# A second group of filler matmuls, and a new set of ranks, in a hand-scheduled attention and feed-forward kernel

## The chip, the core and the metric

The kernel runs on one core of one Trainium2 chip. The metric is the device time of one execution in microseconds; the median of several runs counts. A profile comes from one further execution, taken by the hardware profiler, with its own time.

The engines are named as in the profile: PE is TensorE (matmuls; PEld its weight loads), DVE is VectorE, ACT is ScalarE, POOL is GpSimd, SP is SyncE, which issues loads and stores. Each takes its instructions strictly in the order in which the program was built, and waits where an instruction's inputs or buffers aren't ready.

## What is computed

Attention over selected chunks of keys, and a gated feed-forward network (FFN) on its output, in float32 from and to memory:

```python
# q, k, v: (4, 8, 768, 64); chunks of 32 keys, 24 of them; the best 6 per query
ub = sum_d max(q * k_min[chunk], q * k_max[chunk])     # bound of a chunk, causal chunks only
top = argsort(ub)[..., -6:]
scores = q @ k.T / 8, masked to the keys of `top` and to earlier positions
attn = softmax(scores);  x = (attn @ v) as (3072, 512)
xn = x / rms(x) * rms_g
out = (silu(xn @ w_gate) * (xn @ w_val)) @ w_out       # 512 -> 1536 -> 512
```

## The kernel before

**Pairs.** The 32 heads (4 batches of 8) are taken as 16 pairs of heads, p = 0 to 15; a batch is four pairs. For each pair `prep` loads k and q (`knat`, `qnat`, issued on SP), transposes them on PE (`kT` and `qT`: tiles `pk`, `pq`, L498), copies them out (`kt`, `qt`, on ACT or DVE), reduces the chunks' maxima and minima on DVE (L524, L526, and `ku` on POOL or DVE), multiplies them for the bounds (`ub`, L586), transposes back (`up`, L610), finds the sixth largest bound on DVE (`ubm`, `max`, `selq`, to L644), transposes the selection (`st`, L655) and copies it into the lower rows of the query operand (`qs`). With these rows, and a pattern beside the keys, the score matmul itself adds a large negative number for keys that aren't selected.

**Scores.** `scores` goes through a pair's two heads in groups of at most four 128x128 blocks: score matmuls into PSUM (`sc`, L718, for the first batch with a matmul on a triangular mask, L724), exp on ACT (`pt`, L735), product with v (`av`, L754), and normalisation on DVE into `xb` (L769, L770). The fourth pair (p = 3) is done in two halves of the sequence, so that the first half of the first batch can go on early.

**FFN.** For each half of a batch `norm` takes sums of squares (`sq`, on ACT or DVE), adds epsilon (`ms`, DVE, L810), takes the root on POOL (L818), scales three tiles of 128 rows on DVE (`xs`, L826), and transposes them; in the first batch on PE (`tp`, L848) with a copy by ACT or DVE (`xT`), in the others by DMA. `ffn` then does 12 times a gate matmul (`gp`, four instructions, L882), tanh on ACT (`sg`), a product on DVE (`tg`), a val matmul (`vp`, four instructions, L903) and a product on DVE (`hh`); then nine parts of the output matmul (`po`, four instructions each, L923), evictions and stores. The weights `wg`, `wv` and `wo` are loaded in two halves each, issued on POOL.

**Fillers.** At the start PE has little to do. 48 matmuls of 512 columns on a tile of zeros (`busy`, L341) can be placed there; nobody reads what they write.

**Order.** No scheduler runs on the chip. Before the program is emitted, `Order.run` plays all steps through with estimated durations: at each moment an idle engine takes, among the steps whose inputs and buffers are ready, the one with the lowest rank. The sequence in which the steps were taken is the order of every engine's instructions. A step's rank is a sum: of its kind (the table `RANK`, for the first batch and for the others), of its place (the table `TIMES`: `s3.0` for the scores of the fourth pair's first half, `f0.0` for the first FFN half, and so on) and of a pace times its number within the place. The tables were found by a search. The fillers have rank 1000 and more, behind nearly everything: the planner places one only where PE would have nothing else.

```python
    for i in range(BUSY):
        bank = Buf("ps")
        add("busy", "PE", pe(4 * P), 1000.0 + i, busy(bank), [c_zero], opens=[bank])
```

Of the kernel before, what the change touches and what calls it, by code (L numbers as in the profile page):

```python
# [24 lines left out]

RANK = (
    dict(
        av=156.13, dif=-333.01, eps=-30.9, exp=-297.75, kC=249.04, kE=-171.16, kT=-97.43,
        kload=1.5, kmn=-85.09, kmx=75.56, max=-238.74, qC=324.63, qE=-109.16, qT=-140.07,
        qload=45.82, relu=246.29, root=261.37, sc=129.21, sel=17.88, selC=51.2, selT=55.02,  # L30
        sq=-363.37, tp=-68.78, tpE=108.05, ub=-155.85, ubE=-484.91, ubm=-159.09, up=-350.79,
        vload=-102.18, xb=-100.78, xs=-3.48,
    ),
    dict(
        av=8.1, dif=164.62, eps=-549.11, exp=227.88, gate=-37.01, hh=-145.73, kC=-36.47,
        kE=243.85, kT=-61.3, kload=39.2, kmn=324.05, kmx=284.92, mask=143.91, max=194.96,
        out=-122.32, po=137.5, poE=216.04, qC=234.68, qE=-450.99, qT=88.22, qload=32.32,
        relu=163.99, root=-883.1, sc=-22.64, sel=-113.94, selC=20.01, selT=-328.58, sq=384.43,
        tanh=51.44, tg=-50.58, ub=10.99, ubE=298.61, ubm=-119.37, up=-28.2, val=-0.94,
        vload=151.14, xT=-62.62, xb=39.12, xs=-64.22,  # L40
    ),
)

TIMES = {
# [15 lines left out]
}  # L60


# [139 lines left out]
def kernel(  # L202
# [11 lines left out]
    nc = tc.nc  # L214
    P = nc.NUM_PARTITIONS
# [25 lines left out]
    WHOLE, HALVES = [(0, NT)], [(0, HB), (HB, HB)]  # L241
    PARTS = [WHOLE] * 3 + [HALVES] + [WHOLE] * (NPAIRS - NP)
    FIRST = 42.0
    BUSY = 48
    LIMITS = dict(score=(5, 3), av=(2, 2), prep=(4, 3), ffn=(3, 4), norm=(3, 2), po=(2, 2))
    order = Order(SLOTS, limits)
    order.LIM = LIMITS
# [3 lines left out]
    def add(name, engs, occ, rank, *a, **kw):  # L251
        return order.add(name, engs, occ, rank if isinstance(rank, dict) else {"": rank}, *a, **kw)
# [14 lines left out]
    ps = ctx.enter_context(tc.tile_pool(name="ps", bufs=1, space=PSUM))  # L267
# [11 lines left out]
    def act(n):  # L279
        return 0.065 + n * 0.00083  # L280
# [4 lines left out]
    def pool(n):  # L285
        return 0.22 + n * 0.00085

    def pe(n):
        return 0.003 + n / 2400.0
# [36 lines left out]
    def make_ident(e):  # L326
# [7 lines left out]
        out=first[:], in_=ident_f[:, 0:1], func=ACT.Exp), [c_id])  # L334
    zeros = const.tile([P, 4 * P], BF16, name="zeros")
    c_zero = add("zeros", "DVE", 0.2, -101, lambda e: nc.vector.memset(zeros[:], 0.0))

    def busy(bank):
        def go(e):
            t = tile_of(bank, [P, 4 * P], FP32, "busy")  # L340
            nc.tensor.matmul(t[:], zeros[:, 0:P], zeros[:], start=True, stop=True)  # L341
        return go

    for i in range(BUSY):
        bank = Buf("ps")
        add("busy", "PE", pe(4 * P), 1000.0 + i, busy(bank), [c_zero], opens=[bank])
    c_ku = [add("ku0", "DVE", 0.1, -95 + i, lambda e, i=i: nc.vector.memset(KU[i][:], 0.0))
            for i in range(SLOTS["ku"])]
    c_sel = [add("selq0", "DVE", 0.38, -90 + i, lambda e, i=i: nc.vector.memset(SELQ[i][:], 0.0))
# [52 lines left out]
    def make_tri(e):  # L402
# [10 lines left out]
        out=gains[:], in_=moe_rms_g.rearrange("(o n) -> o n", o=1).to_broadcast([P, DM])),  # L413
# [279 lines left out]
    def scores(c, i0, nb, at, pace, adds):  # L693
        p, b = c.p, c.b
        if b not in XB:
            XB[b], XBS[b] = Buf("xb"), {}
        for hl in range(2):
            kk = slice(0, KM) if hl == 0 else slice(0, P)
            av = Buf("ps", "av")
# [3 lines left out]
            for g, (nd, regions) in enumerate(groups):  # L703
                sc, pt = Buf("ps", "score"), Buf("pt")
                nn = sum(x[2] for x in regions)
                todo, x = [], 0
                for kb, q0, y in regions:
                    todo += [(x + j, kb, q0 + j) for j in range(y)]
                    x += y
                m = g + hl * len(groups)  # L710
                tri = nd if adds else 0

                def score(e, regions=regions, sc=sc, hl=hl, kk=kk, tri=tri):
                    t = tile_of(sc, [P, 4, P], FP32, "sc")
                    ke, qs = KE[c.set.slot][hl], QS[c.set.slot][hl]
                    x = 0
                    for kb, q0, m in regions:
                        nc.tensor.matmul(  # L718
                            t[:, x:x + m, :].rearrange("p a b -> p (a b)"),
                            ke[kk, kb * P:(kb + 1) * P], qs[kk, q0 * P:(q0 + m) * P],  # L720
                            start=not tri or x == 0, stop=not tri)
                        x += m
                    if tri:
                        nc.tensor.matmul(  # L724
                            t[:, 0:tri, :], ident_b[:],
                            trimask[:].rearrange("p (o q) -> p o q", o=1).to_broadcast([P, tri, P]),
                            start=False, stop=True)

                need = list(c.sel) + [y for z in c.ke.values() for y in z] + [c_tri] + c_ke
                s = add("sc", "PE", sum(pe(x[2] * P) for x in regions) + (pe(tri * P) if tri else 0),  # L730
                        rank(at, b, "sc", m, pace), score, need, opens=[sc], uses=[c.set])

                def soft(e, sc=sc, pt=pt, nn=nn):
                    t = tile_of(pt, [P, 4, P], BF16, "pt")
                    nc.scalar.activation(out=t[:, 0:nn, :], in_=sc.tile[:, 0:nn, :], func=ACT.Exp,  # L735
                                         scale=SCALE)

                x = add("exp", "ACT", act(nn * P), rank(at, b, "exp", m, pace), soft, [s], opens=[pt], uses=[sc])
                if nd and not adds:
                    def mask(e, pt=pt, nd=nd):  # L740
                        nc.gpsimd.affine_select(  # L741
                            out=pt.tile[:, 0:nd, :], in_=pt.tile[:, 0:nd, :],
                            compare_op=ALU.is_ge, fill=0.0, base=0,
                            pattern=[[0, nd], [1, P]], channel_multiplier=-1)

                    x = add("mask", "POOL", pool(nd * P), rank(at, b, "mask", m, pace), mask, [x], uses=[pt])

                def prod(e, pt=pt, todo=todo, av=av, left=left, hl=hl):
                    begin = av.tile is None
                    if begin:  # L750
                        tile_of(av, [P, nb, D + 1], FP32, "av")
                    left[0] -= 1
                    for m, (x, kb, qi) in enumerate(todo):
                        nc.tensor.matmul(  # L754
                            av.tile[:, qi - i0, :], pt.tile[:, x, :],
                            VX[c.v.slot][:, hl * NT + kb, :],
                            start=(begin and m == 0), stop=(left[0] == 0 and m == len(todo) - 1))

                avs.append(add("av", "PE", 0.029 * nn, rank(at, b, "av", m, pace), prod, [x, c.vload], opens=[av],
                               uses=[pt, c.v]))  # L760

            def norm_out(e, hl=hl, av=av):
                if XB[b].tile is None:
# [10 lines left out]
            s = add("xb", "DVE", 0.30 + nb * 64 * 0.00104, rank(at, b, "xb", (hl + 1) * len(groups), pace),  # L774
                    norm_out, avs, opens=[XB[b]], uses=[av])
# [210 lines left out]
```

## Time and profile before

| | us |
|---|---|
| median of 3 runs | 325.68 (325.23 to 325.82) |
| the profiled execution | 326.77 |
| its span, first to last instruction | 325.1 |
| mean granted TensorE clock over the span | 0.989 of full |
| first FFN matmul starts | 56.06 |
| last matmul ends | 321.1 |

The page of the profile gives the busy time of each engine, and the span in 40 equal slices of 8.13 us, each digit a tenth; in its row PEclk a 9 is the full granted clock. Busy time of PE includes the latency of each matmul, so two matmuls that follow each other overlap in the records, and a lone one looks longer than what it takes from the array. A view by stretches gives busy time, clock and DMA for chosen windows; the chain of waits follows the work that ended last back from the end, and there a run of matmuls stands with the time that it added; a timeline lists instructions in order, with the idle time before them and its cause in brackets.

### The profile page before, as it was taken

How to read it: one execution, taken by the hardware profiler on the slowest of the kernel's cores; microseconds unless marked ns; L12 is line 12 of the kernel's file. 1: busy time of each engine (PE TensorE's matmuls, PEld its weight loads, DVE VectorE, ACT ScalarE, POOL GpSimd, SP SyncE). 2: the span in 40 equal slices, each digit the busy share in tenths (PEclk: the TensorE clock that was granted, in tenths of full speed). 3: DMA queues.
4: the chain of work that ended last, by engine and by line, in shares of the span. 5: the costliest groups of instructions: out<-in, count | busy, mean ns of one | idle time of the engine just before them, and what ended most of it. 6: DMA issues, size and time to landing. Idle time of an engine off the chain costs nothing.

```text
span 325.1 us, 7875 instructions
## 1 busy us (share of the span) xinstructions
PE 316.8 (97%) x2972; PEld 200.5 (62%) x2972; DVE 245.1 (75%) x664; ACT 201.5 (62%) x434; POOL 118.8 (37%) x170
## 2 busy tenths in 40 slices
PE   8999998999999999999999999999999999999995
PEld 3567865667667767765667667556665466555542
DVE  6789988799789889879998767969767778444500
ACT  5578988575777498993469779755465252333121
POOL 8649426364425764583213556520012000000000
PEclk9999997899999999999999999999999999999999
DMA  9999999798908669857010330150000720011023
GB/s 172 213 216 198 180 198 219 118 191 143 92 0 184 87 106 169 149 140 50 1 50 2 24 28 2 40 123 35 0 2 33 131 65 1 34 65 66 1 79 114
DMA packets 92501, 30.25 MB, mean 93 GB/s; under 512 B 85424, under 2 KB 89264, under 8 KB 92464
## 3 DMA queue, kind: packets, MB, share of 16 engines
q1 hardware_dynamic: 62352, 21.50, 29.8%
q0 software_dynamic: 28512, 7.87, 24.0%
q10 hardware_dynamic: 1600, 0.39, 0.6%
q8 instruction: 23, 0.38, 0.5%
q14 instruction: 14, 0.11, 0.1%
HBM read 28.57 MB, written 6.29 MB: 107 GB/s over the span
## 4 chain that ended last, share of the span: by engine, by line
PE 92%; DVE 4%; DMA 1%; ACT 1%; issue 0%; ACTq 0%
PE gp L882 20%; PE vp L903 19%; PE po L923 19%; PE sc L718 11%; PE av L754 6%; PE ub L586 5%; PE pq L498 3%; PE pk L498 3%; PE busy L341 3%; PE up L610 2%; PE st L655 2%; DMA qnat<-in_q_dram 1%; DVE selq L644 1%; PE tp L848 0%; DVE selq L639 0%
## 5 line engine op out<-in xcount | busy, mean ns | idle before, releaser
L735 ACT ACTIVATE pt<-sc 128x512 bf16<-128x512 f32 (+3 forms) x192 | 90.9, 570 | 7.4 <-PE sc L718 5.2
L889 ACT ACTIVATE sg<-gp 128x384 bf16<-128x384 f32 x96 | 46.9, 493 | 53.1 <-PE gp L882 52.3
L882 PE MATMUL gp<-xT,wg 128*128 128x384 bf16 x384 | 76.1, 331 | 0.0
L903 PE MATMUL vp<-xT,wv 128*128 128x384 bf16 x384 | 75.7, 326 | 0.0
L895 DVE SCALAR_TENSOR_TENSOR tg<-sg,gp 128x384 bf16<-128x384 bf16 x96 | 51.7, 550 | 25.7 <-ACT sg L889 24.8
L923 PE MATMUL po<-wo,hh 128*128 128x512 bf16 x288 | 69.2, 379 | 0.0
L911 DVE TENSOR_TENSOR hh<-vp,tg 128x384 bf16<-128x384 f32 x96 | 52.3, 553 | 9.7 <-PE vp L903 8.6
L718 PE MATMUL sc<-qs,ke 89*128 89x128 bf16 (+5 forms) x420 | 56.7, 256 | 0.5 <-ACT qs L294 0.4
L882 PEld LDWEIGHTS <-wg 128*128 128x128 bf16 x384 | 36.9, 99 | 25.2 <-issue 2.4
L903 PEld LDWEIGHTS <-wv 128*128 128x128 bf16 x384 | 36.0, 98 | 23.1 <-issue 0.8
L741 POOL TENSOR_SCALAR_AFFINE_SELECT pt<-pt 128x512 bf16<-128x512 bf16 (+1 forms) x48 | 26.1, 556 | 63.3 <-ACT pt L735 62.8
L923 PEld LDWEIGHTS <-hh 128*128 128x128 bf16 x288 | 27.3, 98 | 26.7
L754 PE MATMUL av<-vx,pt 128*128 128x65 bf16 x672 | 38.9, 193 | 1.3 <-ACT pt L735 1.3
L754 PEld LDWEIGHTS <-pt 128*128 128x128 bf16 x672 | 32.4, 98 | 10.6 <-ACT pt L735 2.2
L718 PEld LDWEIGHTS <-ke 89*128 89x128 bf16 (+1 forms) x420 | 30.9, 99 | 10.2 <-issue 2.1
L298 POOL CAST qs<-qt 64x768 bf16<-64x768 f32 x30 | 28.3, 944 | 24.3 <-DVE qt L298 13.3
L298 POOL CAST ke<-kt 64x768 bf16<-64x768 f32 x31 | 26.5, 855 | 8.3 <-ACT kt L294 5.9
L296 ACT ACTIVATE osb<-po 128x512 f32<-128x512 f32 x19 | 11.3, 597 | 29.2 <-PE po L923 29.2
L294 ACT ACTIVATE qs<-st 64x768 bf16<-64x768 bf16 x20 | 16.1, 804 | 7.5 <-PE st L655 7.2
L826 DVE SCALAR_TENSOR_TENSOR xs<-xb,ri,gains 128x512 bf16<-128x512 bf16 x24 | 18.3, 797 | 1.5 <-DMA xT<-xs 1.0
L770 DVE TENSOR_TENSOR xb<-av,rden 128x384 bf16<-128x384 f32 (+1 forms) x34 | 18.2, 534 | 1.2
L631 DVE MAX8 m<-ubm 128x8 f32<-128x24 f32 x192 | 18.9, 169 | 0.1
(72 smaller groups left out, 335.8 us busy)
## 6 DMA issues: line engine op xcount, KB each, us to landing
out_dram<-osb SPq DMA_DIRECT2D x24, 256.0 KB, 2.2
knat<-in_k_dram SPq DMA_DIRECT2D x30, 192.0 KB, 4.8
qnat<-in_q_dram SPq DMA_DIRECT2D x30, 192.0 KB, 4.9
vx<-in_v_dram POOLq DMA_DIRECT2D x16, 192.0 KB, 5.2
wo<-in_moe_w_out_dram POOLq DMA_DIRECT2D x2, 768.0 KB, 9.3
wg<-in_moe_w_gate_dram POOLq DMA_DIRECT2D x2, 768.0 KB, 8.8
wv<-in_moe_w_val_dram POOLq DMA_DIRECT2D x2, 768.0 KB, 9.3
ke<-e_all SPq DMA_DIRECT2D x4, 96.0 KB, 3.4
```

Source lines behind the costliest of these rows:

```text
L298: engine[e].tensor_copy(out_, in_)
L498: nc.tensor.transpose(t[:, j * P:(j + 1) * P], nat[w].tile[:, j0 + j].rearrange("p h d -> p (h d)"), ident_f[:])
L718: nc.tensor.matmul(t[:, x:x + m, :].rearrange("p a b -> p (a b)"), ke[kk, kb * P:(kb + 1) * P], qs[kk, q0 * P:(q0 + m) * P], start=not tri ...
L735: nc.scalar.activation(out=t[:, 0:nn, :], in_=sc.tile[:, 0:nn, :], func=ACT.Exp, scale=SCALE)
L741: nc.gpsimd.affine_select(out=pt.tile[:, 0:nd, :], in_=pt.tile[:, 0:nd, :], compare_op=ALU.is_ge, fill=0.0, base=0, pattern=[[0, nd], [1, ...
L754: nc.tensor.matmul(av.tile[:, qi - i0, :], pt.tile[:, x, :], VX[c.v.slot][:, hl * NT + kb, :], start=(begin and m == 0), stop=(left[0] == ...
L882: nc.tensor.matmul(t[:], wg[:, g, hs], XT[b].tile[:, g, cols], start=(g == 0), stop=(g == NP - 1))
L889: nc.scalar.activation(out=t[:], in_=gp.tile[:], func=ACT.Tanh, scale=0.5)
L895: nc.vector.scalar_tensor_tensor(out=t[:], in0=sg.tile[:], scalar=1.0, in1=gp.tile[:], op0=ALU.add, op1=ALU.mult)
L903: nc.tensor.matmul(t[:], wv[:, g, hs], XT[b].tile[:, g, cols], start=(g == 0), stop=(g == NP - 1))
L911: nc.vector.tensor_tensor(out=t[:], in0=vp.tile[:], in1=tg.tile[:], op=ALU.mult)
L923: nc.tensor.matmul(po.tile[:], hhs[ht].tile[:, th * P:(th + 1) * P], wo[:, ht, :], start=(ht == 0), stop=(ht == NHT - 1))
```

## The change

There are two parts. After the scores of the third pair (p = 2) forty more matmuls on zeros are offered to the planner, of 256 columns each. They depend on the pair's last score step and on nothing else, have the same ranks of 1000 and more as the first group, and each takes a PSUM bank for the time that it runs. And both rank tables hold new numbers, from a new search with these forty in place; by them every engine's order changes from the second pair on. All steps are the same; the eviction copies that either ACT or DVE may do are shared out differently.

```diff
 RANK = (
     dict(
-        av=156.13, dif=-333.01, eps=-30.9, exp=-297.75, kC=249.04, kE=-171.16, kT=-97.43,
+        av=144.2, dif=-491.58, eps=80.61, exp=-371.37, kC=299.85, kE=4.76, kT=-114.77,
...
 TIMES = {
-    "a0": -160.49, "a1": -10.55, "a10": 206.64, "a11": 125.99, "a12": 264.8, "a13": 190.02,
+    "a0": -265.54, "a1": 7.97, "a10": 278.72, "a11": 147.3, "a12": 324.93, "a13": 250.5, "a14":
...
-    BUSY = 48
+    BUSY, LATER = 48, 40
...
-    def busy(bank):
+    def busy(bank, n):
         def go(e):
             t = tile_of(bank, [P, 4 * P], FP32, "busy")
-            nc.tensor.matmul(t[:], zeros[:, 0:P], zeros[:], start=True, stop=True)
+            nc.tensor.matmul(t[:, 0:n], zeros[:, 0:P], zeros[:, 0:n], start=True, stop=True)
         return go
...
-        add("busy", "PE", pe(4 * P), 1000.0 + i, busy(bank), [c_zero], opens=[bank])
+        add("busy", "PE", pe(4 * P), 1000.0 + i, busy(bank, 4 * P), [c_zero], opens=[bank])
...
-                s = add("sc", "PE", sum(pe(x[2] * P) for x in regions) + (pe(tri * P) if tri else 0),
+                s = last_sc = add("sc", "PE", sum(pe(x[2] * P) for x in regions) + (pe(tri * P) if tri else 0),
                         rank(at, b, "sc", m, pace), score, need, opens=[sc], uses=[c.set])
...
+            if p == 2 and hl:
+                for i in range(LATER):
+                    bank = Buf("ps")
+                    add("busy", "PE", pe(2 * P), 1000.0 + i, busy(bank, 2 * P), [last_sc], opens=[bank])
```

More of the change, by code (lines that the diff above doesn't have):

```diff
@@ L27 @@
     dict(
-        av=156.13, dif=-333.01, eps=-30.9, exp=-297.75, kC=249.04, kE=-171.16, kT=-97.43,
[L29 to L32, printed above, removed]
+        av=144.2, dif=-491.58, eps=80.61, exp=-371.37, kC=299.85, kE=4.76, kT=-114.77,
+        kload=9.63, kmn=30.2, kmx=-28.41, max=-225.53, qC=341.63, qE=-85.17, qT=-65.07,
+        qload=37.04, relu=227.01, root=185.03, sc=127.33, sel=95.16, selC=107.08, selT=-124.54,
+        sq=-359.31, tp=-102.27, tpE=5.42, ub=-213.91, ubE=-563.24, ubm=167.25, up=-358.34,
+        vload=-60.34, xb=-160.93, xs=-122.34,
     ),
     dict(
[L35 to L40, printed above, removed]
+        av=-11.76, dif=-2.19, eps=-312.61, exp=84.27, gate=-33.95, hh=-312.21, kC=-56.83,
+        kE=197.29, kT=-62.54, kload=46.97, kmn=412.42, kmx=172.58, mask=54.76, max=242.91,
+        out=-348.43, po=91.59, poE=382.1, qC=107.93, qE=-401.84, qT=31.34, qload=43.39,
+        relu=98.28, root=-755.08, sc=-47.74, sel=57.49, selC=-254.04, selT=-245.0, sq=236.73,
+        tanh=185.25, tg=-53.7, ub=-43.58, ubE=291.78, ubm=15.41, up=-21.92, val=-11.75,
+        vload=304.71, xT=30.46, xb=28.85, xs=-150.44,
     ),
```

28 rows, old and new, of the table TIMES are left out of this document.

## The prediction

> **What bounds the kernel now.** I read the page first: which engine is full, and where its clock was not.
>
> ```profile
> span 325.1 us, 7875 instructions
> PE 316.8 (97%) x2972; PEld 200.5 (62%) x2972; DVE 245.1 (75%) x664; ACT 201.5 (62%) x434; POOL 118.8 (37%) x170
> PEclk9999997899999999999999999999999999999999
> ```
>
> TensorE (PE) is busy 97% of the span, and the granted clock falls in one place only, the seventh and eighth of the 40 slices (48.8 to 65.0 us). The busy time by stretches narrows that down; after the stretch's length come the busy time of PE, PEld, DVE, ACT and POOL, each with its count, then the clock, the DMA share and GB/s.
>
> ```profile
> 48.00:49.00 1.00, 0.44 (x7) 0.15 (x3) 0.77 (x5) 1.00 (x6) 0.00 (x1) 1.00 1.14 199
> 49.00:50.00 1.00, 0.56 (x7) 0.32 (x7) 0.97 (x4) 1.00 (x4) 1.00 (x2) 1.00 1.16 202
> 50.00:51.00 1.00, 0.60 (x8) 0.36 (x9) 1.00 (x3) 0.54 (x2) 0.94 (x2) 1.00 1.16 202
> 51.00:52.00 1.00, 0.87 (x10) 0.62 (x11) 1.00 (x2) 0.45 (x1) 1.00 (x1) 1.00 1.16 202
> 52.00:53.00 1.00, 0.63 (x8) 0.59 (x7) 1.00 (x2) 0.98 (x2) 1.00 (x2) 0.62 1.16 201
> 53.00:54.00 1.00, 1.00 (x6) 0.51 (x5) 0.47 (x1) 1.00 (x3) 0.01 (x1) 0.50 1.15 211
> 54.00:58.00 4.00, 4.00 (x23) 2.58 (x22) 2.49 (x8) 3.85 (x10) 1.64 (x3) 0.50 1.25 239
> 58.00:59.00 1.00, 1.00 (x5) 0.48 (x4) 0.55 (x1) 0.21 (x2) 0.24 (x1) 0.50 1.15 200
> 59.00:60.00 1.00, 1.00 (x8) 0.57 (x7) 0.55 (x1) 0.80 (x3) 0.00 (x0) 0.97 1.15 201
> 56.06:60.00 3.94, 3.94 (x17) 1.96 (x16) 2.31 (x6) 2.95 (x9) 0.87 (x1) 0.62 1.17 208
> 60.00:305.56 245.56, 245.56 (x2282) 156.50 (x2281) 196.11 (x508) 152.45 (x333) 83.21 (x114) 1.00 0.41 68
> ```
>
> From 48 to 53 us PE idles 0.56 + 0.44 + 0.40 + 0.13 + 0.37 = 1.90 us. The clock then goes to half and stays there until 59: lost time 0.38 + 0.50 + 2.00 + 0.50 + 0.03 = 3.41 us, 3.94 x 0.38 = 1.50 us of it after 56.06. From 60 us to the final stretch PE never idles. So after the feed-forward part (FFN) starts, at 56.06, the end is a matter of PE work alone; before it, of the chain that feeds the first gate. The chain that ended last and the engines' timelines (start, length) show that chain:
>
> ```profile
> 49.14 0.27 PE L754 MATMUL av<-vx,pt 128*128 128x65 bf16 x3 [0.70 <-ACT pt L735]
> 51.64 0.40 PE L848 MATMUL tp<-ident_b,xs 128*128 128x128 bf16 x4
> 52.41 1.86 PE L718 MATMUL sc<-qs,ke 89*128 89x128 bf16 x10 [0.37 <-ACT qs L294]
> 54.92 0.63 PE L848 MATMUL tp<-ident_b,xs 128*128 128x128 bf16 x4
> 56.06 4.22 PE L882 MATMUL gp<-xT,wg 128*128 128x384 bf16 x16
> 305.56 15.55 PE po L923 x72
> 48.74 0.17 DVE L810 TENSOR_SCALAR ms<-ss 128x3 f32<-128x3 f32 x1 [0.23 <-ACT junk L797]
> 50.84 2.63 DVE L826 SCALAR_TENSOR_TENSOR xs<-xb,ri,gains 128x512 bf16<-128x512 bf16 x3
> 55.59 0.42 DVE L298 COPY xT<-tp 128x512 bf16<-128x512 bf16 x1
> 53.08 0.58 ACT L294 ACTIVATE xT<-tp 128x512 bf16<-128x512 bf16 x1
> ```
>
> The three scaled rows (xs) are done at 53.47, yet the third transpose (tp) starts only at 54.92, behind scores at half clock, its copy ends at 56.01, and the gate starts at 56.06. PE ends at 321.1; evicting and storing the last tile takes the remaining 4.0 us, in either kernel.
>
> **The added work.** Forty 256-column matmuls on zeros, with no reader. Neighbours in the chain of waits:
>
> ```profile
> 13.43 1.95 PE busy L341 x9
> 21.28 0.11 PE sc L724
> 92.91 0.89 PE sc L718 x10
> 98.08 0.66 PE pq L498 x6
> 24.30 0.33 PE st L655 x6
> 28.26 1.17 PE av L754 x38
> ```
>
> A 512-column zero matmul takes 1.95 / 9 = 0.217 us, a 256-column mask matmul 0.11, so one new one costs 0.109 and forty 4.36 us of PE. PE takes its instructions in order: "ranked last" decides only where each is put when the program is built. The built order has 11 of them (1.2 us) in groups of 2 to 4 between the last av groups of the third pair (p = 2), ahead of the fourth pair's first scores; the other 29 (3.16 us) from behind the fourth pair's up transposes to its third tp. None is behind the first gate. So 4.36 us must fit into the time before the FFN.
>
> For the 29: the stretch 48 to 53 has at least the 1.90 us of recorded idle. The most is what is left of 48.1 to 52.4 when only array time counts: 15 av at 1.17 / 38, six st at 0.33 and four tp at 0.055 each make 1.0 of 4.3 us, so 3.3. The recorded waits of 0.19 to 0.70 us before each av group have the next exp as their end, and a matmul's record includes its latency; I take 3.0, nearer the upper end. For the 11: the exps give the rhythm.
>
> ```profile
> 53.56 2.04 ACT L735 ACTIVATE pt<-sc 128x512 bf16<-128x512 f32 x4
> 42.18 1.12 DVE L298 COPY qs<-st 64x768 bf16<-64x768 bf16 x2
> ```
>
> One exp per 0.51 us; four av (0.12) with two to four zero matmuls (0.22 to 0.44) take 0.34 to 0.56. What follows them, the fourth pair's scores, waited in the trace for the two qs copies on DVE, which end at 43.30. DVE is the cover; without it the 11 cost up to 1.2 us.
>
> **The order.** I summed the built orders up to the first FFN matmul. Six pq transposes (0.66) and score matmuls with 1,664 columns (the ten of 0.89 us have 8 x 128 + 2 x 512 = 2,048, so 0.72) now stand behind it: 1.38 us that PE must do later, at a time when it has no idle. On DVE the queue up to the third xs has three qt copies less, one kt and one ubs copy more: some 0.48 x 3 - 0.48 - 0.34 = 0.6 us less. (A 128x384 copy follows the next after 0.48 us in this row.)
>
> ```profile
> 23.57 1.02 DVE L298 COPY qt<-pq 128x384 f32<-128x384 f32 x2 [0.32 <-PE pq L498]
> ```
>
> So xs can end at 53.47 - 0.6 = 52.9. Behind the third xs there is now only its tp (0.40) and an ACT copy (0.58); the nine scores that stand between (0.66 at full clock) run beside the copy. With 0.1 for handing over, the first FFN matmul could start at 54.0. PE could be the later one: from the fourth pair's first score to the third tp the new order has 9.7 us of array time (3.16 of it zeros). From about 43.0 (the 43.30 of the copies, less part of the 0.6) that ends at 52.7 if nothing waits, 0.6 us ahead of the chain; with a few waits for exps of some 0.3 us each it ends a little behind it. I take 54.3.
>
> Other queues. On POOL the first wg half moves behind ku, which itself stands behind the qs copies; both wv halves go early and both wo halves late.
>
> ```profile
> 40.54 0.94 DVE L526 TENSOR_REDUCE ku<-kt 128x24 f32<-128x768 f32 x1
> 41.98 0.23 POOL L542 TENSOR_TENSOR ku<-kmx,ku 128x24 f32<-128x24 f32 x1 [2.62 <-DVE rden L769]
> 42.43 0.79 POOL L420 DMA_DIRECT2D wg<-in_moe_w_gate_dram  x1 [0.21 <-issue]
> DMA to landing us min/median/max: 7.0/8.8/11.6
> ```
>
> With the copies done at about 42.8, ku on DVE ends at 43.7, on POOL at about 44.0, and the load is issued at 44.1. It lands at 51.1 to 55.7, 52.9 at the median, and is needed at 54.3 + 0.65 (one val comes first). Cost nothing, at worst 0.8 us. The second wg half, right behind the root, is needed six gates and four vals later: covered. SP loads the same tiles in a changed order, q ahead of k; the loads for the first pk and pq behind the start wait only for transposes of the second pair, long done.
>
> **The sum.** FFN start 56.06 to 54.3: -1.76. Half clock behind the start: -1.50. Work moved behind it: +1.38. Together -1.9 us: 326.77 to 324.9 for the profiled execution (span 325.1 and 1.7 around it). The runs' median, 325.68, lies 1.09 lower, at 323.8. Measurement can tell about 0.2% (0.65 us) from no change.
>
> **Why the clock should hold.** It fell right behind four microseconds in which PE was busy for 0.44 to 0.87, and much of that is latency (1.0 us of array time in 4.3). In the new order the part from the first of the 29 to the third tp holds 5.3 us of array time for some 6.5 us. [...] The rows have 6.4 us at half speed, with PE full from 53.0, so I keep 3.41.
>
> **Rivals.**
> 1. The zeros don't fit (slower). If only the recorded 1.90 us of idle takes them, 4.36 - 1.90 = 2.5 us go on the chain to the first gate: start 54.0 + 2.5 = 56.5, less 1.50, plus 1.38: +0.3, and with the 11 also delaying DVE up to +1: 326.0 to 326.7. It decides from a start at 56.2 on (56.06 + 1.50 - 1.38). For: PE's margin is 0.6 us. Against: hidden idle in the records. 11%.
> 2. The clock falls all the same, as it would if light load were not its cause. The start is then at about 55.7 behind half-speed transposes and zeros, the clock is back at 59 as before, 1.38 is added: +1.0, 326.7. 7%. [...]
> 3. New waits in the 265 us behind the start: an order searched anew must feed PE without a gap for all that time, as the old one does. Work per engine and total is nearly unchanged (DVE +1 us). One wait of an exp's length per 60 us would be 2 us: 325.8. 10%, most of it no change.
> 4. The first wg half lands last: +0.8, 324.6, still faster. Part of the forecast.
>
> **How the numbers follow.** Forecast 72%: 323.8, its own range 322.9 (start at 53.4, the DVE gain twice 0.6 and PE ahead of it) to 325.0 (start at 55.5). Rivals 1 and 2 are slower; of 3, 2% are faster, 7% the same, 1% slower. Faster 0.74, same 0.07, slower 0.19. The range goes from 322.6 (a start at 53.1) to 326.2: above it are left rival 2 and the worse half of 1, some 12%, below it few.
>
> **What would show it.** Right: PEclk 1.00 from 48 to 60; the first FFN matmul at 53.8 to 54.8; L341 with 88 instructions and hardly a wait on it; no PE idle behind it; PE's end near 319.2. Wrong: half clock anywhere; a start behind 56.2; PE idle of over 1 us behind 60 us; a gate waiting for wg.

## The result, and the profile after

The changed kernel takes 325.25 us, the median of 22 runs (324.57 to 326.70); the kernel before takes 326.15 us on the same chip (22 runs, 325.23 to 326.93). The ratio is 0.9975, 95% interval 0.9964 to 0.9986. That is 0.9 us between the medians, where the forecast had 1.9. The profiled execution took 326.38 us, one of the longer ones. Lines of its page:

```profile
span 324.7 us, 7959 instructions
PE 316.6 (98%) x2988; PEld 203.4 (63%) x3012; DVE 248.0 (76%) x668; ACT 203.7 (63%) x429; POOL 117.8 (36%) x171
PEclk9999999999999999999999999999999999999999
```

The dent in PEclk is gone. By stretches (columns as before):

```profile
48.00:53.00 5.00, 5.00 (x72) 4.15 (x69) 4.73 (x23) 4.22 (x11) 1.65 (x2) 1.00 1.15 207
53.00:56.00 3.00, 2.63 (x33) 2.13 (x32) 2.92 (x9) 2.97 (x5) 0.00 (x0) 1.00 1.15 208
56.00:60.00 4.00, 4.00 (x26) 2.42 (x25) 2.11 (x6) 3.63 (x10) 3.23 (x5) 1.00 0.96 188
```

PE is full from 48 to 53 us, and the granted clock reads 1.00 throughout. Now the waits of PE, all of them from 5 us to the end (engine, line, who was late: us in total, times, longest):

```profile
PE av L754 <- DMA vx<-in_v_dram: 1.0, 1, 1.0
PE vp L908 <- ACT xT L294: 0.4, 1, 0.4
PE st L655 <- DVE selq L644: 0.2, 1, 0.2
```

Behind the start of the FFN there is no wait at all, as forecast. The first line is new: the kernel before never waited for a load of `v`. The timeline of PE places it:

```profile
20.86 1.09 PE L718 MATMUL sc<-qs,ke 128*128 128x128 bf16 x9
29.60 1.22 PE L754 MATMUL av<-vx,pt 128*128 128x65 bf16 x34 [1.03 <-DMA vx<-in_v_dram]
55.65 0.81 PE L908 MATMUL vp<-xT,wv 128*128 128x384 bf16 x4 [0.37 <-ACT xT L294]
312.81 7.93 PE L928 MATMUL po<-wo,hh 128*128 128x512 bf16 x35
```

The first FFN matmul starts at 55.65, not at 54.3, and PE ends at 312.81 + 7.93 = 320.74. The same marks in the kernel before:

```profile
20.19 1.09 PE L718 MATMUL sc<-qs,ke 128*128 128x128 bf16 x9
28.10 1.33 PE L754 MATMUL av<-vx,pt 128*128 128x65 bf16 x38
```

So two things had gone against the changed kernel in this execution before 30 us, far ahead of the zeros: the first score matmul came 0.67 us later (20.86 against 20.19; the last section says why this is no effect of the change), and the first product with `v` followed it after 8.74 us instead of 7.91. The chain of waits names the second:

```profile
20.68 8.87 DMA vx<-in_v_dram
29.60 1.22 PE av L754 x34
```

At 20.7 us two `v` tiles are asked for, and the first pair's products need the first of them. It took 8.87 us to land. In the kernel before, the same two landed sooner (the view of the tile, 15 to 30 us; here the smallest number is the first load's):

```profile
DMA to landing us min/median/max: 6.3/7.0/7.6
```

What had moved beside them is on SP's queue; first before, then after:

```profile
16.77 0.84 SPq L412 DMA_DIRECT2D gains<-in_moe_rms_g_dram  x1
```

```profile
20.92 0.74 SPq L412 DMA_DIRECT2D gains<-in_moe_rms_g_dram  x1
```

The 256 KB load of the gains went out 3.2 us ahead of the `v` loads before (20.01), and 0.2 us behind the first of them after.

### The profile page after: what moved, and what is told of

Same layout as the page of the kernel before. It is cut to its first block, busy times and chain, and to the rows that moved or that the text cites. A ratio compares the mean times of both kernels' runs of the same rounds, so it can differ in the third digit from the quotient of the medians.

```text
span 324.7 us, 7959 instructions
## 1 busy us (share of the span) xinstructions
PE 316.6 (98%) x2988; PEld 203.4 (63%) x3012; DVE 248.0 (76%) x668; ACT 203.7 (63%) x429; POOL 117.8 (36%) x171
## 4 chain that ended last, share of the span: by engine, by line
PE 92%; DMA 3%; ACT 2%; DVE 1%; issue 1%; POOL 0%; ACTq 0%; POOLq 0%
PE vp L908 19%; PE gp L887 19%; PE po L928 19%; PE sc L718 10%; PE av L754 6%; PE ub L586 4%; PE busy L341 4%; PE pk L498 3%; PE pq L498 3%; DMA vx<-in_v_dram 3%; PE up L610 2%; PE st L655 1%; ACT pt L735 1%; PE sc L724 1%; PE tp L853 0%
## 5 line engine op out<-in xcount | busy, mean ns | idle before, releaser
L908 PE MATMUL vp<-xT,wv 128*128 128x384 bf16 x384 | 77.0, 326 | 0.4 <-ACT xT L294 0.4
L928 PE MATMUL po<-wo,hh 128*128 128x512 bf16 x268 | 66.7, 379 | 1.1
L718 PE MATMUL sc<-qs,ke 128*128 128x128 bf16 (+4 forms) x417 | 55.3, 250 | 0.0
L298 POOL CAST qs<-qt 64x768 bf16<-64x768 f32 x30 | 27.3, 911 | 45.2 <-ACT qt L294 34.4
L754 PE MATMUL av<-vx,pt 128*128 128x65 bf16 x672 | 41.0, 194 | 1.2 <-DMA vx<-in_v_dram 1.0
L754 PEld LDWEIGHTS <-pt 128*128 128x128 bf16 x672 | 33.6, 98 | 12.3 <-DMA vx<-in_v_dram 1.5
L718 PEld LDWEIGHTS <-ke 89*128 89x128 bf16 (+1 forms) x420 | 30.0, 97 | 8.5 <-issue 1.6
L294 ACT ACTIVATE qs<-st 64x768 bf16<-64x768 bf16 x26 | 20.9, 805 | 5.9 <-PE st L655 5.5
L296 ACT ACTIVATE osb<-po 128x512 f32<-128x512 f32 x19 | 11.5, 605 | 20.7 <-PE po L928 20.6
L341 PE MATMUL busy<-zeros 128*128 128x512 bf16 (+1 forms) x87 | 20.9, 358 | 1.3 <-DVE zeros L336 1.3
```

Source lines behind the costliest of these rows:

```text
L298: engine[e].tensor_copy(out_, in_)
L341: nc.tensor.matmul(t[:, 0:n], zeros[:, 0:P], zeros[:, 0:n], start=True, stop=True)
L718: nc.tensor.matmul(t[:, x:x + m, :].rearrange("p a b -> p (a b)"), ke[kk, kb * P:(kb + 1) * P], qs[kk, q0 * P:(q0 + m) * P], start=not tri ...
L754: nc.tensor.matmul(av.tile[:, qi - i0, :], pt.tile[:, x, :], VX[c.v.slot][:, hl * NT + kb, :], start=(begin and m == 0), stop=(left[0] == ...
L908: nc.tensor.matmul(t[:], wv[:, g, hs], XT[b].tile[:, g, cols], start=(g == 0), stop=(g == NP - 1))
L928: nc.tensor.matmul(po.tile[:], hhs[ht].tile[:, th * P:(th + 1) * P], wo[:, ht, :], start=(ht == 0), stop=(ht == NHT - 1))
```

## The experiments

**The `v` load in time.** In either order the first `v` load, issued at about 9 us, fills a tile that is read only at 33 us, and the tile needed first is loaded second. The edit exchanges the two:

```diff
+    loads = [i for i, s in enumerate(done) if s.name == "v"]
+    done[loads[0]], done[loads[1]] = done[loads[1]], done[loads[0]]
     for s in done:
         s.emit(s.eng)
```

In the changed kernel:

> The changed kernel with one edit: the first two loads of v change places in the order that is emitted, so that the v tile that pair 0's weighted sums read is asked for at about 8.7 us instead of 20.7 us; everything else, the 40 zeros included, is left. Theory (the gain was cut by the 1.03 us in which TensorE waited at 29.6 us for that v tile, which landed 9.8 us after its issue where the kernel before saw 7.0 us): that wait goes, the first FFN matmul starts near 54.6 us instead of 55.65 us, and the time falls by about 1.0 us, to about 324.2 us where the changed kernel has 325.25. Rival (the wait only stands for a late DMA queue, and the next late load takes its place, or another chain was as late): the first FFN matmul stays within 0.3 us of 55.65 us and the time within 0.3 us of the changed kernel's.

Measured: 325.41 us (12 runs), ratio to the kernel before 0.9970 (0.9952 to 0.9989). (The 9.8 and 7.0 us of the expectation are medians of the two loads; the one that PE waited for took 8.87 us, and 6.3 in the kernel before.) In the trace all went as the theory had it: no wait for `v`, first FFN matmul at 54.70, 0.95 us earlier. The expected 324.2 us was not reached: the ratio is hardly below the 0.9975 of the changed kernel, which was timed apart from this run, beside a kernel before at 326.15 where it read 326.58 here.

The control in the kernel before:

> The kernel before with the same exchange of its first two v loads, as a control. There TensorE did not wait for that v tile (its weighted sums began at 28.10 us with no DMA wait). Theory: no change, 326.15 us within 0.4 us. Rival (the early place of that load is worth something by itself, whatever the zeros do): about 1 us faster here too.

Measured: 326.58 us, ratio 1.0008 (0.9990 to 1.0027). No change, as expected: here the tile was not late.

**The wait again.** The changed kernel once more, unaltered:

> The changed kernel itself, unaltered, as the yardstick on this chip and for a second profile. Theory (the late v tile is no accident of the first profiled execution but follows from the order of the loads): TensorE waits again 0.5 to 1.6 us for it near 29.6 us and the first FFN matmul starts near 55.0 to 55.7 us; median 325.2 to 325.7 us. Rival (an accident of that one execution): no wait over 0.3 us, first FFN matmul at 54.5 to 54.8 us.

Measured: 325.66 us, ratio 0.9979 (0.9962 to 0.9996). The wait is there again, longer:

```profile
29.05 1.22 PE L754 MATMUL av<-vx,pt 128*128 128x65 bf16 x34 [1.12 <-DMA vx<-in_v_dram]
55.11 0.81 PE L908 MATMUL vp<-xT,wv 128*128 128x384 bf16 x4 [0.37 <-ACT xT L294]
```

**The gains earlier.** On the same chip:

```diff
+    gain = done.pop(next(i for i, s in enumerate(done) if s.name == "gains"))
+    done.insert([i for i, s in enumerate(done) if s.name == "qload"][5], gain)
```

> The changed kernel with one load moved: the 256 KB load of the gains is issued ahead of the fifth q load, its place in the kernel before (about 17 us), instead of behind the fourth pair of k loads (20.9 us, beside the two v loads issued at 20.7 us). Theory (the gains load in the same microsecond is what makes the v tile land 8.9 to 9.8 us after its issue instead of 7.0): the wait at 29.6 us shrinks by 0.8 us or more, the first FFN matmul starts near 54.7 us, time 0.3 to 1.0 us below the changed kernel's on the same chip. Rival (all queues are full there and it only matters how many bytes are ahead): the v tile lands within 0.4 us of where it did, or a q or k tile is late in its place; time within 0.3 us.

Measured: 325.59 us, ratio 0.9968 (0.9955 to 0.9981). The two `v` tiles asked for at 21.0 us landed as before the change:

```profile
DMA to landing us min/median/max: 6.7/7.2/7.8
```

The wait is gone. One profile is thin evidence, for the changed kernel itself met no such wait in one of its three profiles (further below). All 17 profiles together say more. In six the gains went out 3.1 to 3.8 us ahead of the two `v` loads, in the five of the old order and in this one: the first of the two took 6.0 to 6.7 us. In the other eleven they went out 0.2 to 1.4 us behind it, and it took 6.5 to 9.4 us. So late gains make a late tile likely, not certain. The medians of the two kernels differ by 0.07 us only, where 0.3 to 1.0 was expected. The slowest execution fell from 327.21 to 326.00, but what the move is worth in the median stayed open here.

**Without the 40 zeros.** The changed order, the later zeros not emitted:

```diff
+    later = [s for s in done if s.name == "busy"][BUSY:]
+    left_out = set(later[:])
     for s in done:
-        s.emit(s.eng)
+        if s not in left_out:
+            s.emit(s.eng)
```

> The changed kernel's order with the 40 later zero matmuls not emitted and nothing else touched; the output doesn't depend on them. Theory (the zeros keep the clock up): the granted clock falls to half somewhere in 45 to 60 us as in the kernel before, 1.5 to 3.4 us are lost to that, the zeros' 4.36 us of TensorE work fell mostly into idle time, so the time is 1 to 3 us above the changed kernel's, 326.3 to 328.3 us. Rival (the denser order of the real work, found anew, keeps the clock up, and the zeros only fill waits): the clock stays at 1.00 and the time is the changed kernel's within 0.4 us, or below it by up to 1 us if some zeros push the chain.

Measured: 325.84 us, ratio 0.9986 (0.9962 to 1.0010). That is less than the 326.3 to 328.3 that was expected. In 7 of the 12 executions the mean clock was below 0.997 (mean time 326.38 us), in 5 it was not (325.23); with the zeros and the exchange, on the same chip, it was below in none of 12. So the zeros do hold the clock. But the new order alone loses it only in part of its executions, and for a shorter time (3.41 us at half clock in the profile, 1.71 lost).

The same with the `v` loads exchanged, beside the exchange with the last 29 zeros:

> The changed kernel with the first two v loads exchanged and none of the 40 later zeros (the output doesn't depend on them): the new order without the late tile and without the zeros. Theory (the zeros keep the clock up; without them it falls in part of the executions): granted clock 0.995 in about half of the executions, those 1 us slower than the rest; median 0.4 to 1.0 us above v_last29_b on the same chip. Rival (the zeros are not needed once the v tile is in time): clock 1.00 in nearly all, median within 0.3 us of v_last29_b.

> The exchange and the last 29 zeros once more, beside v_none. Theory (it is the version that has both what the forecast counted on): 324.8 us, ratio to the kernel before 0.9955 to 0.9965, so that the forecast's -1.9 us is nearly reached; first FFN matmul at 54.0 to 54.7 us. Rival (the 7 runs of the first time were lucky ones): 325.3 us or more.

Measured on one chip: 325.25 us without zeros (7 runs, ratio 0.9948, 0.9927 to 0.9968), 324.64 us with 29 (6 runs, ratio 0.9940, 0.9921 to 0.9959). Without zeros the clock fell in 4 of 7 executions, 325.55 us in the mean against 324.68 for the other three, which are as fast as those with zeros. So, as far as seven runs tell, the zeros cost nothing there and a fall costs about 0.9 us. The kernel before stood at 326.65 us on this chip: with the tile in time, 1.4 of the 2.0 us came from the new order without any zeros. The profile without zeros caught one, by stretches:

```profile
52.00:53.00 1.00, 0.70 (x9) 0.45 (x8) 1.00 (x4) 0.97 (x2) 0.00 (x0) 0.92 1.24 267
53.00:54.00 1.00, 1.00 (x12) 1.00 (x10) 0.93 (x4) 1.00 (x3) 0.00 (x0) 0.50 1.29 264
54.00:55.00 1.00, 1.00 (x6) 0.41 (x4) 0.88 (x4) 1.00 (x5) 0.00 (x0) 0.50 1.19 221
55.00:56.00 1.00, 1.00 (x5) 0.44 (x3) 0.17 (x1) 1.00 (x5) 0.35 (x1) 0.50 1.17 214
56.00:57.00 1.00, 1.00 (x7) 0.55 (x6) 0.00 (x0) 0.67 (x3) 1.00 (x3) 0.87 1.18 217
```

Lost: 0.08 + 0.50 + 0.50 + 0.50 + 0.13 = 1.71 us, just half of the 3.41 lost in the first profile.

**Zeros without the new order.** Into the kernel before, by hand, 18 zero matmuls of 256 columns, three at each of six places between 48 and 53 us (the choice of places and PSUM banks is left out here):

```diff
...
+    zeros_before = {**{s: 3 for s in avs}, **{s: 3 for s in sts}, tps[0]: 3}
     for s in done:
+        for _ in range(zeros_before.get(s, 0)):
+            zero_at(at[s])
         s.emit(s.eng)
```

> The kernel before, its order untouched, with 18 zero matmuls of 256 columns put in by hand: 3 ahead of each of the last four weighted sums of the third pair's last group, 3 ahead of the transposes of the state, 3 ahead of the first transposes behind them (48 to 53 us). Theory (the half-speed stretch of 52.6 to 59 us is lost because TensorE is idle too often in 48 to 53 us): the clock stays at 1.00, the first FFN matmul starts near 54.2 us or a little later, and the time falls by 1.5 to 3.4 us, to 322.7 to 324.7 us. Rival (the zeros push the chain, or the clock falls anyway): 326 to 328 us, with the granted clock below 1 in 52 to 59 us.

Measured: 326.76 us, ratio 1.0011 (0.9990 to 1.0032). The mean clock was 0.997 or more in all 12 executions, and yet no time was gained, where 1.5 to 3.4 us were expected. PE's timeline, this kernel and then the one before, at the same gates and at the same bounds:

```profile
63.45 3.42 PE L882 MATMUL gp<-xT,wg 128*128 128x384 bf16 x20
70.81 0.38 PE L718 MATMUL sc<-qs,ke 128*128 128x512 bf16 x1 [0.94 <-DVE hh L911]
71.12 0.80 PE L586 MATMUL ub<-qt,ku 64*32 64x256 f32 x12
```

```profile
65.33 3.41 PE L882 MATMUL gp<-xT,wg 128*128 128x384 bf16 x20
71.51 0.65 PE L586 MATMUL ub<-qt,ku 64*32 64x256 f32 x12
```

At the gates PE is 1.88 us ahead; at the bounds it is 0.39 ahead, having waited 0.94 us for DVE's `hh` and 0.17 for its `tg`. In the old order DVE stood close behind PE there, which a PE without idle time doesn't show. Some of the gain was missing earlier: the first FFN matmul came at 55.65, not near 54.2. The first profile lost 1.91 us to the clock ahead of it (3.41 - 1.50), and only 0.79 of that came back, counted from the first score (55.65 - 20.57 against 56.06 - 20.19). Whether the 18 zeros pushed the rest is not shown.

**The kernel before at another clock.** Two further profiles:

> The kernel before, for another profile. Among its executions so far 30 of 65 had a mean clock of 0.990 or less (mean time 326.95 us), 18 one of 0.991 to 0.996 (325.6 us), 17 one of 0.997 or more (326.4 us). Theory (the stretch at half clock is not of the same length in every execution, so that the first profile showed its costliest case): in an execution at 0.993 the stretch is about 2 us shorter, at 0.999 it is missing, and the later layers then wait for VectorE, as with the zeros put into this order by hand. Rival (the fall is the same each time and the three clocks come from elsewhere): the half-speed stretch is there at 52.6 to 59 us in each.

> The same as b_look1, a further execution of the kernel before, to meet another of its three clocks.

Measured: 326.30 us at a mean clock of 0.992, 326.23 us at 0.993. The first by stretches:

```profile
53.00:54.00 1.00, 0.63 (x8) 0.59 (x7) 1.00 (x2) 0.97 (x2) 1.00 (x2) 0.67 1.16 201
54.00:55.00 1.00, 1.00 (x6) 0.52 (x5) 0.47 (x1) 1.00 (x3) 0.01 (x1) 0.50 1.16 205
55.00:56.00 1.00, 1.00 (x8) 0.77 (x7) 0.26 (x1) 1.00 (x4) 0.71 (x2) 0.50 1.25 279
56.00:57.00 1.00, 0.99 (x11) 0.87 (x9) 0.96 (x5) 0.84 (x3) 0.29 (x1) 0.62 1.34 246
```

Lost: 0.33 + 0.50 + 0.50 + 0.38 = 1.71 us again, in the same program that lost 3.41 in the first profile. At half speed that is a stretch of 3.4 us where the first had 6.8; expected was one about 2 us shorter. No execution of this kernel without a fall was caught in a profile.

**The first 11 zeros, and the late tile in the median.** First without the 11 zeros at 42 to 44 us, in the edit above `later[:11]` left out:

> The changed kernel without the first 11 of its 40 later zeros (those ahead of pair 4's first scores, 42 to 44 us); the output doesn't depend on them. Theory (the 29 behind them, in 48 to 54 us, keep the clock up; the 11 stand where TensorE would wait for the qs copies anyway): clock 1.00 throughout, time within 0.3 us of the changed kernel's. Rival A (the 11 count too): the clock falls in some executions as without any of the 40, +0.3 to +1 us in the median. Rival B (the 11 push the scores): 0.3 to 1.2 us faster.

> The exchange of the first two v loads and the last 29 zeros only, together. Theory: the exchange takes the wait for the v tile away where it occurs (about 0.2 us in the median by the two medians so far, 1 us in an execution that has the wait) and the 11 zeros are free: 0 to 0.5 us below the changed kernel on the same chip, with the clock at 1.00. Rival (without the 11 the clock falls): as a_last29's rival A, 0.3 to 1 us above.

Measured on one chip: 326.08 us (ratio 0.9992, 0.9977 to 1.0007), and with the exchange 324.78 us (7 runs, ratio 0.9958, 0.9941 to 0.9975). The clock held in both. Against the unaltered changed kernel there (325.66) the one looked slower, the other faster, so three kernels went together onto one chip:

> The changed kernel itself once more, beside the two below on one chip. Theory (the late v tile costs it about 1 us in most executions): median 0.5 to 1.1 us above v_full_c, with the wait of 0.3 us or more for the v tile in its profile. Rival (the exchange is worth little, as the 0.25 us between the two medians on different chips suggested): within 0.3 us of v_full_c.

> The exchange of the first two v loads with all 40 later zeros, on the same chip as the other two. Theory (the 11 zeros at 42 to 44 us fill waits and cost nothing): within 0.2 us of v_last29_c. Rival (they push pair 4's scores): 0.3 to 0.8 us above v_last29_c, and the first FFN matmul that much later counted from the weighted sums at about 28 us.

> The exchange with the last 29 zeros only, on the same chip. Theory and rival as for v_full_c; time 324.6 to 325.0 us, ratio to the kernel before 0.994 to 0.996.

| 12 runs each | median, us | ratio to before | 95% interval |
|---|---|---|---|
| the changed kernel | 326.12 | 0.9989 | 0.9966 to 1.0013 |
| `v` loads exchanged | 325.20 | 0.9961 | 0.9943 to 0.9979 |
| and without the first 11 zeros | 325.19 | 0.9964 | 0.9945 to 0.9984 |

Side by side, the exchange is worth 0.92 us in the median, the 11 zeros nothing. Over all their runs the changed kernel stood at 0.9975, 0.9979 and 0.9989 of the kernel before, and the exchanged one at 0.9970 and 0.9961, which is anything from 0.2 to 0.9 us: the sign is surer than the size. One expectation failed: the changed kernel's own profile had no wait for `v` this time. The tile took 7.8 us there, from its issue at 21.37, and so landed just ahead of the first product at 29.19. The exchange with 29 zeros is the fastest version found: 0.9940 to 0.9964 of the kernel before in three comparisons.

## Why the forecast was only half right

**Where the work went: right.** No half clock, no PE idle behind the start, and from the start to PE's end 320.74 - 55.65 = 265.09 us; the forecast's own numbers, 319.2 - 54.3, make 264.9. So -1.50 for the clock and +1.38 for the moved work hold as a sum, to 0.2 us, and the clock shows the first of them directly. The wg half, issued at 45.55 instead of 44.1, made nobody wait.

**The first FFN matmul at 54.3: right for the chain that was summed, wrong in the trace.** The step that failed is "Other queues", where SP's changed order of loads was costed at nothing: only loads near the FFN were looked at, not what the order does to a load on another queue at 20 us. From the first score to the first product with `v` an undisturbed execution takes 7.64 us (28.51 - 20.87 with the loads exchanged, 27.81 - 20.17 in the lines below). That leaves 7.8 us for a load issued 0.2 us ahead of the score; the tile took 8.87 us, where it took 6.3 before. Cost: 1.1 us in the profile (8.74 - 7.64); in the median 0.92 where both kernels ran side by side, 0.2 to 0.9 over all pairs.

In the profile the start came 1.35 us behind the forecast (55.65 against 54.3): 1.10 for the tile and 0.67 for the later first score, less 0.42 by which the rest of the chain was shorter than forecast. So part of that miss was chance, and the chain was a little better than it was costed.

With the tile in time, and a first score as early as in the profile of before, the timeline reads:

```profile
20.17 1.09 PE L718 MATMUL sc<-qs,ke 128*128 128x128 bf16 x9
27.81 1.22 PE L754 MATMUL av<-vx,pt 128*128 128x65 bf16 x34
53.88 0.81 PE L908 MATMUL vp<-xT,wv 128*128 128x384 bf16 x4 [0.37 <-ACT xT L294]
311.03 7.93 PE L928 MATMUL po<-wo,hh 128*128 128x512 bf16 x36
```

That is the exchange with 29 zeros: start at 53.88, PE's end at 318.96, profiled execution 324.59. The forecast had 54.3, 319.2 and 324.9. With all 40 zeros and the exchange the start was at 54.70 and 54.69 in the two profiles, each with a first score at 20.87.

**The profile as the base: one case of three.** The sum took the 3.41 us of the first profile for what every execution loses. In 106 executions of the kernel before, timed beside the experiments, 49 had a mean clock of 0.990 or less (mean 326.96 us), 30 one of 0.991 to 0.996 (325.48), and 27 one of 0.997 or more (326.39). Against the fastest version's mean of 324.97 (25 executions, all at 0.997 or more), the first group gives -2.0, the forecast's case; the others give -0.5 and -1.4. Taking -1.9 off a median that mixes the three was wrong by some tenths of a microsecond: the groups' weighted mean is -1.4. That the first profile stood 1.09 us above the median of the runs shown could have warned of it. That median itself was of three runs: 325.68, where 22 gave 326.15, so 0.47 of the 1.45 us between 323.8 and 325.25 is in the starting point. How the other 0.98 divides between the tile and the groups is not measured.

**Why the clock should hold: right.** With the zeros no execution of any version, new order or old, had a mean clock below 0.997: none of 131, where 79 of 106 of the kernel before were below it. In the first profile the clock fell at 52.24 us, and from 48 us on PE had no wait longer than 0.70 us. With 18 zeros put into these short waits of the old order it was below 0.997 in none of 12. So a fall came behind waits of 0.19 to 0.70 us, and none came once zeros filled them; how much load it takes to prevent one is not shown.

The 3.41 us that the forecast kept as the loss is right for the first profile. (It read 6.4 us at half speed from its rows; they give 6.8, twice its own 3.41.) It is not right for every execution: the two profiles of the kernel before at a mean clock of 0.992 and 0.993 lost 1.71 us, and as far as the mean clock tells, that is the case of 30 of the 106.

**The rivals.** 1: the zeros fit; with 11 fewer nothing is gained. 2: did not occur. 3: no new wait behind the start in the new order, but the mechanism is real in the old one, where 1.88 us gained at the gates shrank to 0.39 at the next bounds. So zeros alone, as they were placed there, brought nothing in the old order; that no other placing would is not shown. The measured 325.25 lies inside the range, for a reason that was not among the rivals.

What stays open: why executions of the kernel before without a fall (326.39) are slower than those with a short one (325.48). The give-back to DVE fits the first; none was profiled. And the two profiles with a short fall are no typical cases of theirs: 326.30 and 326.23 us, above all 30 timed executions of that group (324.91 to 326.14).

## What to carry to other kernels

When an order is searched anew, follow every load whose place changed to the loads of other queues that fly beside it, and compare each one's time to landing with the time until its first reader, as early as it lies. Before taking a stall off a median, see whether the runs' mean clocks fall into groups; one profile shows one of them. A gain on a saturated engine can be given back at the next engine, as 1.88 us shrank to 0.39 here: test it by putting the cure alone into the old order.

## What the runs showed of the hardware

The stretches at half clock came in two lengths. The six profiles with a fall lost 1.71 us (four, in both orders) or 3.41 us (two, both in the old order) to it. The kept traces also hold the entries from which the clock in the views is made, and these show when a fall comes (times in us from the start of the span):

| profile | first entry at full clock | half clock from | for |
|---|---|---|---|
| before, `v` exchanged | 4.23 | 52.01 | 6.83 |
| before, the first | 4.45 | 52.24 | 6.83 |
| changed, `v` exchanged, no zeros | 5.05 | 52.84 | 3.41 |
| before, another | 5.55 | 53.34 | 3.41 |
| before, a third | 6.08 | 53.86 | 3.41 |
| changed, no zeros | 6.61 | 54.40 | 3.41 |

Each fall begins 47.78 to 47.79 us behind the first entry, and a long one, 6.83 us, is twice a short one. The first entry lies differently in each execution: between 4.23 and 6.61 us in the table, at 7.28 in the first profile of the changed kernel, which has no fall. In the old order the length of the fall goes with it: long at 4.23 and 4.45, short at 5.55 and 6.08. That could make the three groups of the kernel before; whether its executions without a fall have a later first entry is not shown, as none was profiled. A last entry at half clock stands behind the last matmul and delays none: it begins at 324.72 us in the first profile of the changed kernel, where PE ends at 320.74, and at 322.5 in the one with the `v` loads exchanged and no zeros, where PE ends before 321. In the latter it takes 0.95 us off the 324.4 of the span, three thousandths of the mean clock, which is why a mean of 0.997 can be an execution without a fall.

The first score came between 20.08 and 21.55 us in 17 profiles, in either order; part of that is the pace of the first matmuls. PE's timeline of the kernel before, then of the changed one:

```profile
5.18 0.38 PE L341 MATMUL busy<-zeros 128*128 128x512 bf16 x1
6.25 1.03 PE L341 MATMUL busy<-zeros 128*128 128x512 bf16 x4
```

```profile
5.50 0.63 PE L341 MATMUL busy<-zeros 128*128 128x512 bf16 x1
6.56 1.39 PE L341 MATMUL busy<-zeros 128*128 128x512 bf16 x4
```

The same 512-column matmul takes 0.38 us at 5.2 us in the one and 0.63 us at 5.5 us in the other, with the same instructions ahead of it, and the granted clock reads 1.00 there in both. The entries of the clock begin at 4.45 us in the one and at 7.28 in the other; where there is none yet, the views show 1.00. Ahead of the first entry such a matmul takes 0.61 to 0.63 us in both profiles, behind it 0.38, and the one that runs across it (from 6.99 us, in the second) 0.53. The other part is the k load behind it, for which PE waited 0.4 to 0.7 us near 16 us in some profiles of either order and not at all in others. The two profiles shown here had no such wait. Their next transposes start at 7.12 and 7.79 us: the whole 0.67 us between their first scores is there already, behind the same instructions. The first entry lay at 4.45, 5.55 and 6.08 us in three executions of the kernel before, unaltered, so the 0.67 us is put down to chance and not to the change.
